# The second product for tiles 0 and 1 of the first unit: seven block products instead of eight, with the weights' block sums made earlier and in other places

## The chip, the cores and the metric

The kernel runs on one NeuronCore of one Trainium2 chip. The core has five engines with queues of their own: TensorE (PE in the profile; PEld is its weight load) multiplies matrices into PSUM, VectorE (DVE), ScalarE (ACT) and GpSimd (POOL) work elementwise, and SyncE (SP) mostly issues transfers. Each queue runs in its written order: an instruction that waits holds all behind it. The metric is the device time of one execution in microseconds (us), as the median of several runs.

## The reference

The input holds q, k and v of 8 batches, 12 heads, 448 rows and 64 columns. Attention without a softmax is followed by a feed-forward layer:

```python
scores = scale * np.matmul(q, k.transpose(0, 1, 3, 2))
attn = np.maximum(scores, 0.0) ** 2 / S
x = matmul(attn, v)              # heads side by side: B x 448 x 768
xn = (x - mu) / np.sqrt(var + 1e-06) * g_ln
out = x + np.maximum(xn @ w_ch1, 0.0) @ w_ch2     # 768 -> 3072 -> 768
```

All is given and returned in float32; the kernel multiplies in bf16.

## The kernel before, in words

**Attention.** A batch is done in three periods, n = 3 b + 0..2, of four heads each. A period has seven score steps s = 0..6 (`att_QK`, L584: four matmuls of 64x448 into one of three PSUM slots), a relu that empties the slot (L593 on ScalarE or L595 on VectorE), a square in place (L608 on VectorE, L610 on POOL), and then AV (`att_AV`, L645, 28 matmuls), whose result is copied as x transposed (L363 on ScalarE, L365 on VectorE). POOL adds x up for the mean (`sum_part`, L734 to L737), one matmul with ones makes the mean (`center`, L816), ScalarE saves it (L829), and VectorE subtracts it (L837) and applies the gain (L846; ScalarE L844).

**First product of the layer, `ffn_1`.** 24 steps for a batch, each six matmuls of 128x448 (L926) into one of two PSUM banks. A relu writes h (L942 on ScalarE, L944 on VectorE). For the second batch (b = 1) each relu is two instructions, of 64 and 384 columns, since part of h lies in a buffer called A (its first half, for tiles 4 to 6) and B (its second).

**Second product.** A unit is two batches, 896 rows in seven tiles of 128; tile 3 takes rows of both batches. For a tile `ffn_2` does two column halves of 384, each a sum of 24 matmuls of 128x384 (L1212), which VectorE drains with the row's scale and the residual x (L1230) and ScalarE's queue stores. The first unit's tiles are all done so, in the order 4, 5, 6, 3, 0, 1, 2, after `ffn_1` of the second batch, with the attention of batch 2 (periods 6 to 8; below: one to three) put in between.

In later units the pairs (0, 1), (3, 4) and (5, 6) use seven block products instead of eight (`ffn_w`, L1122): h of two tiles is a 2 x 2 block matrix a11..a22 (tile by half of the 3072), w2 one of b11..b22. Each product is 12 matmuls of 128x384, made in the order P1 = a11 b11, P2 = a12 b21, P6 = S2 T2, P5 = S1 T1, P7 = S3 T3, P3 = S4 b22, P4 = a22 T4. The S are differences of h, made for each pair by VectorE (`s_op`, L1079: S3 = a21 - a11 in place, S2 = a22 - S3 in a home of its own, S1 and S4 in place of a11 and a12), two instructions each. The T are sums of w2's blocks, made once (`make_sums`, L989: T3 = b22 + b12, T2 = T3 - b11, T4 = b21 - T2, T1 = b12 - b11), 12 blocks of 384 columns each. The order of the drains (L1130) is fixed by the sums they make: P1, P2, P6, P5, P7, P3 and P4 each have one.

Homes in the kernel before: T3 and the first two blocks of T2 in buffer A, the rest of T2 in the freed v buffer and the freed input of `ffn_1` of batch 0 (`v0`, `xc0`), T4 in `xc0`, behind the transposed x (`xT_all`) and in `x_all[:, 6]`, which is tile 2's residual; T1 in the k half of the staging buffer `stage["cols"]` and at the end of `at_all`. S2 lies in `x_all[:, 4:6]`, the residual of tiles 0 and 1.

**What sets the order.** Every operation goes to `Order`, a planner in the kernel's text. It has a modelled cost and wait for each operation; TensorE's order is set by `segment`, which interleaves steps of the layer with visits of attention, and the other engines' operations are placed in modelled time by readiness and then by `key` (lower first). An operation with two engines goes to the one that would end it first. What results is a fixed queue for each engine; on the chip nothing is reordered. `hooks` in `segment` are calls made when a given step is reached: loads of batch 3 at step 0, its transposes (`turn_qk`, SP, L414) and `make_sums` at step 24 + 32, that is after four tiles. POOL's queue also issues the loads of q, k (L401) and v (L385), SP's the transposes of x (L764). `later` and `now_known` name an operation that is added afterwards.

Of the kernel before, what the change touches and what calls it, by code (L numbers as in the profile page):

```python
# [199 lines left out]
def kernel(  # L200
# [10 lines left out]
    nc = tc.nc  # L211
    P = 128
# [5 lines left out]
    B, H, S, D = q.shape  # L218
# [15 lines left out]
    FIRST_ORDER = "qqaqaqqqqqqaaaqaqaaqaqaqqqaaaqaaqaaqqaaqqaaaaaaaa"  # L234

# [156 lines left out]
    def load_qk_cols(b):  # L392

        free = [ops["qk_free", 0]] if b == 2 else [later("turn", b - 1, x) for x in range(2)]
        for t, src in enumerate((q, k)):
# [588 lines left out]
    def make_sums():  # L984

        def run(o, i0, i1, sub, deps, key):
            def emit(eng):
                e = nc.vector if eng == "DVE" else nc.gpsimd
                (e.tensor_sub if sub else e.tensor_add)(o, i0, i1)  # L989
            n = o.shape[1] * hd  # L990
            return R.add(("DVE", "POOL"), (100.0 + 0.55 * n, 120.0 + 2.05 * n), emit, deps, key=key, port=True)

        wide = lambda t, n: t.rearrange("p (k c) -> p k c", c=hd)[:, :n]
        homes = []
        a_t = big_pool.tile([P, BIG], bf16, tag="A")
        v_t = v_pool.tile([P, H // 2, S], bf16, tag="v0")
        c_t = xc_pool.tile([P, K1, S], bf16, tag="xc0")
        homes = [(a_t[:, :14 * hd], 14, [ops["f2_end", 1]]),
                 (v_t.rearrange("p a c -> p (a c)"), 7, []), (c_t.rearrange("p a c -> p (a c)"), 7, []),
                 (xT_all[:, 4 * d_model:], 6, [ops[x, bb] for x in ("x_read", "turn_x") for bb in range(2)]),  # L1000
                 (x_all[:, 6, :], 2, [later("f2_out", 0)])]
        space = [(v.rearrange("p (k c) -> p k c", c=hd)[:, i:i + 1], d) for v, n, d in homes for i in range(n)]
        free = [(v.rearrange("p (k c) -> p k c", c=hd), n, d) for v, n, d in homes]
        made = {}

        def place(name):

            k, out = 0, []
            while k < KH:
                v, n, d = free.pop(0)  # L1010
                w = min(n, KH - k)
                out.append((k, v[:, :w], d))
                for i in range(w):
                    tw[name, k + i] = v[:, i]
                if w < n:
                    free.insert(0, (v[:, w:], n - w, d))
                k += w
            return out

        def pieces(runs):  # L1020
            for k, v, d in runs:
                n = v.shape[1]
                for i in range(0, n, 3):
                    yield k + i, v[:, i:min(i + 3, n)], d
        t3, t2, t4 = place("T3"), place("T2"), place("T4")
        w2_ld = [ops["w2", K2 - 1]]
        for k, o, d in pieces(t3):
            made["T3", k] = run(o, b22[:, k:k + o.shape[1]], b12[:, k:k + o.shape[1]], False, w2_ld + d, 5.0)
        done3 = [op for (x, _), op in made.items() if x == "T3"]
        for k, o, d in pieces(t2):  # L1030
            for i in range(o.shape[1]):
                made["T2", k + i] = run(o[:, i:i + 1], tw["T3", k + i].rearrange("p (o c) -> p o c", o=1),
                                        b11[:, k + i:k + i + 1], True, done3 + d, 5.1)
        for k, o, d in pieces(t4):
            for i in range(o.shape[1]):
                made["T4", k + i] = run(o[:, i:i + 1], b21[:, k + i:k + i + 1],
                                        tw["T2", k + i].rearrange("p (o c) -> p o c", o=1), True, [made["T2", k + i]] + d, 5.2)
        at_end = at_all[:, (N_AT - 1) * 2 * S:].rearrange("p (k c) -> p k c", c=hd)
        for a, z in ((0, 3), (3, 5), (5, J), (J, 10), (10, KH)):
            o = stage["cols"][:, 1, a:z] if a < J else at_end[:, a - J:z - J]  # L1040
            for k in range(a, z):
                tw["T1", k] = o[:, k - a]
            made["T1", a] = run(o, b12[:, a:z], b11[:, a:z], True, w2_ld + [later("turn", 3, 1), later("av_done", 1)], 5.3)
        for name in ("T1", "T2", "T3", "T4"):
            ops["sums", name] = [op for (x, _), op in made.items() if x == name]

    s2_t = x_all[:, 4:6, :].rearrange("p m (k c) -> p (m k) c", c=P)
# [21 lines left out]
    def s_op(u, m, name, part, deps):  # L1069
# [3 lines left out]
        a1, a2 = tile_cols(u, m), tile_cols(u, m + 1)  # L1073
        a11, a12, a21, a22 = h1[:, k, a1], h1[:, k_hi, a1], h1[:, k, a2], h1[:, k_hi, a2]
# [7 lines left out]
    def pair_start(u, m):  # L1082
# [5 lines left out]
        for part in range(2):  # L1088
            e["S2"].append(s_op(u, m, "S2", part, [e["S3"][part], later("h", b, KH + (part + 1) * KH // 2 - 1),
                                                   later("s2_free", u, m), later("f2_out", 0)]))  # L1090

    def ffn_w(u, m, name, part):
# [13 lines left out]
        if final and name == "P4":  # L1106
            last_product(u, m, part, e, r2, deps)
            return
# [411 lines left out]
```

## Time and profile before

| | |
|---|---|
| median of 5 runs | 525.45 us (525.43 to 525.57) |
| the profiled execution's own time | 525.45 us |
| its span, first to last instruction | 523.6 us |
| TensorE busy | 510.7 us, 98% of the span, 4104 matmuls |
| VectorE, ScalarE, POOL busy | 348.8, 220.3, 115.8 us |
| granted TensorE clock | 0.999 of full speed |

Two readings help with what follows. A matmul's duration in a row (326 ns for 128x384) is longer than its pace, because matmuls overlap; the chain's pieces give the pace. And an engine's instructions overlap a little too: two squares of 0.61 us each take 1.15.

### The profile page before, as it was taken

How to read it: one execution, taken by the hardware profiler on the slowest of the kernel's cores; microseconds unless marked ns; L12 is line 12 of the kernel's file. 1: busy time of each engine (PE TensorE's matmuls, PEld its weight loads, DVE VectorE, ACT ScalarE, POOL GpSimd, SP SyncE). 2: the span in 40 equal slices, each digit the busy share in tenths (PEclk: the TensorE clock that was granted, in tenths of full speed). 3: DMA queues.
4: the chain of work that ended last, by engine and by line, in shares of the span. 5: the costliest groups of instructions: out<-in, count | busy, mean ns of one | idle time of the engine just before them, and what ended most of it. 6: DMA issues, size and time to landing. Idle time of an engine off the chain costs nothing.

```text
span 523.6 us, 9887 instructions
## 1 busy us (share of the span) xinstructions
PE 510.7 (98%) x4104; PEld 277.1 (53%) x4104; DVE 348.8 (67%) x647; ACT 220.3 (42%) x350; POOL 115.8 (22%) x130
## 2 busy tenths in 40 slices
PE   5899999999999999999999999999999999999996
PEld 3444455555555455554555545554556545555564
DVE  5988647538996768774888667748597666634253
ACT  5977611115404663265422664346531466114300
POOL 6421600401263112321250311503221002100000
PEclk9999999999999999999999999999999999999999
DMA  9999999996299901999059960989224400242022
GB/s 188 197 188 194 199 189 165 172 126 108 61 154 146 102 2 19 165 127 106 15 103 113 125 78 15 150 111 100 41 46 88 88 1 0 54 78 22 2 60 62
DMA packets 144281, 51.83 MB, mean 99 GB/s; under 512 B 121830, under 2 KB 142188, under 8 KB 144236
## 3 DMA queue, kind: packets, MB, share of 16 engines
q0 software_dynamic: 81072, 25.50, 45.9%
q1 hardware_dynamic: 55804, 14.79, 18.6%
q10 hardware_dynamic: 7360, 10.92, 8.6%
q8 instruction: 32, 0.52, 0.4%
q14 instruction: 13, 0.11, 0.1%
HBM read 51.91 MB, written 11.01 MB: 120 GB/s over the span
## 4 chain that ended last, share of the span: by engine, by line
PE 95%; DVE 2%; ACT 1%; DMA 1%; issue 0%; ACTq 0%; DVEq 0%
PE f_ps L926 42%; PE f_ps L1122 23%; PE f_ps L1212 15%; PE sc L584 7%; PE ps L645 5%; DVE at_all L608 1%; ACT at_all L593 1%; DVE t L365 1%; DMA f<-in_q_dram 1%; PE ps L504 1%; PE f_ps L906 0%; PE f_ps L1187 0%; PE ps L707 0%; PE f_ps L504 0%; PE slot L816 0%
## 5 line engine op out<-in xcount | busy, mean ns | idle before, releaser
L926 PE MATMUL f_ps<-a,w 128*128 128x448 bf16 x1134 | 220.6, 353 | 0.0
L926 PEld LDWEIGHTS <-w 128*128 128x128 bf16 x1134 | 108.2, 98 | 107.2 <-issue 9.4
L593 ACT ACTIVATE at_all<-sc 128x896 bf16<-128x896 f32 x109 | 95.9, 924 | 78.8 <-PE sc L584 71.9
L942 ACT ACTIVATE h<-f_ps 128x448 bf16<-128x448 f32 (+1 forms) x157 | 83.6, 533 | 107.2 <-PE f_ps L926 105.7
L608 DVE TENSOR_TENSOR at_all<-at_all 128x896 bf16<-128x896 bf16 x158 | 99.5, 666 | 1.9 <-ACT at_all L593 1.8
L1122 PEld LDWEIGHTS <-h 128*128 128x128 bf16 x636 | 61.5, 98 | 42.7 <-issue 2.2
L595 DVE TENSOR_SCALAR at_all<-sc 128x896 bf16<-128x896 f32 x50 | 54.4, 1088 | 42.5 <-PE ps L645 23.2
L1212 PE MATMUL f_ps<-w,h 128*128 128x384 bf16 x336 | 56.3, 326 | 0.0
L1122 PE MATMUL f_ps<-w,h 128*128 128x384 bf16 x324 | 56.2, 326 | 0.0
L584 PE MATMUL sc<-t 64*64 64x448 bf16 x672 | 49.1, 366 | 3.0 <-DVE t L365 1.5
L1212 PEld LDWEIGHTS <-h 128*128 128x128 bf16 x336 | 32.4, 98 | 22.6 <-issue 1.5
L736 POOL TENSOR_TENSOR sum_t<-sum_t,xT_all 128x384 f32<-128x384 f32 (+2 forms) x25 | 21.5, 861 | 86.3 <-ACT xT_all L363 86.3
L584 PEld LDWEIGHTS <-t 64*64 64x64 bf16 x672 | 18.6, 107 | 27.7 <-issue 19.1
L1130 DVE SCALAR_TENSOR_TENSOR o_all<-f_ps,r_t,x_all 128x384 f32<-128x384 f32 x35 | 21.5, 614 | 16.8 <-PE f_ps L1122 16.5
L401 POOL DMA_DIRECT2D t<-in_k_dram x12 | 20.0, 1902 | 50.6 <-DMA t<-t 50.6
L645 PE MATMUL ps<-at_all,v_t 64*64 64x448 bf16 x552 | 29.8, 350 | 0.0
L734 POOL TENSOR_TENSOR sum_t<-xT_all 128x384 f32<-128x384 bf16 (+2 forms) x13 | 11.2, 906 | 84.1 <-ACT xT_all L363 83.9
L1230 DVE SCALAR_TENSOR_TENSOR o_all<-f_ps,r_t,x_all 128x384 f32<-128x384 f32 x20 | 12.3, 613 | 24.6 <-PE f_ps L1212 24.6
L363 ACT CAST xT_all<-ps 128x768 bf16<-128x768 f32 (+2 forms) x31 | 19.7, 641 | 21.2 <-PE ps L645 13.3
L645 PEld LDWEIGHTS <-v_t 64*64 64x64 bf16 x672 | 19.7, 107 | 13.4 <-issue 2.8
L401 POOL DMA_DIRECT2D t<-in_q_dram x12 | 19.3, 1772 | 31.3 <-DMA t<-t 30.0
L1130 DVE SCALAR_TENSOR_TENSOR o_all<-f_ps,r_t,o_all 128x384 f32<-128x384 f32 x27 | 16.6, 615 | 13.7 <-PE f_ps L1122 13.6
(98 smaller groups left out, 420.8 us busy)
## 6 DMA issues: line engine op xcount, KB each, us to landing
out_dram<-o_all ACTq DMA_DIRECT2D x70, 96.0 KB, 2.2
v_t<-in_v_dram POOLq DMA_DIRECT2D x16, 336.0 KB, 6.4
w<-in_moe_w_ch_dram POOLq DMA_DIRECT2D x4, 1152.0 KB, 38.5
t<-in_q_dram POOLq DMA_DIRECT2D x12, 336.0 KB, 8.3
t<-in_k_dram POOLq DMA_DIRECT2D x12, 336.0 KB, 6.8
out_dram<-o_all ACTq DMA_DIRECT2D x20, 192.0 KB, 4.6
w<-in_moe_w_ch_dram POOLq DMA_DIRECT2D x4, 768.0 KB, 19.1
w<-in_moe_w_ch_dram POOLq DMA_DIRECT2D x1, 1536.0 KB, 28.8
```

The costliest lines, as they stand in the source:

```text
L401: nc.gpsimd.dma_start(stage["cols"][half * T:(half + 1) * T, t if b < 4 else 0].rearrange("p j (h d) -> p j h d", d=D), src[b, half * 6:ha ...
L584: nc.tensor.matmul(sc[rows_of(half), r, :S], qkT[b][rows_of(r), 1, s * NPER + pn, rows_of(half)], qT[:, :, pn, rows_of(half)], start=True, ...
L593: nc.scalar.activation(attn[n, s], st[0][:, :, :S], Act.Relu, scale=rc2)
L595: nc.vector.tensor_scalar(attn[n, s], st[0][:, :, :S], rc2, 0.0, op0=Alu.mult, op1=Alu.max)
L608: nc.vector.tensor_mul(attn[n, s], attn[n, s], attn[n, s])
L645: nc.tensor.matmul(av_st[n][half][rows_of(hh)], vt[b][rows_of(half), 2 * pn + hh, s * D:(s + 1) * D], attn[n, s][rows_of(half), hh, :], st ...
L736: nc.gpsimd.tensor_add(s0, s0, x0)
L926: nc.tensor.matmul(st[0], w1[:, ki, ni * P:(ni + 1) * P], xc[b][:, ki, :], start=(i == 0), stop=(i == K1 - 1))
L942: nc.scalar.activation(o, st[0][:, c], Act.Relu)
L1122: nc.tensor.matmul(e["ps", bank], a(k), w(k), start=new and k == 0, stop=k == KH - 1, skip_group_check=True)
L1130: nc.vector.scalar_tensor_tensor(o, e["ps", bank], r, o if more else xm[u, m + tile_n][:, cols], op0=Alu.mult, op1=Alu.add)
L1212: nc.tensor.matmul(o_st["ps"], stat(u, m, ki), w2[:, ki, j * hd:(j + 1) * hd], start=(ki == 0), stop=(ki == K2 - 1))
```

## The change: what it does

1. Tiles 0 and 1 of the first unit are done as a pair with seven products, after tiles 4, 5, 6, 3 and 2. `pair_start(0, 0)` adds S3 and S2 at step 24 + 24, after tile 6.
2. The T are made in two parts. Part 0 is added at step 12 of `ffn_1` of the second batch: T3 in `v0` and `xc0`, T1's last five blocks, T2's first eight (one in each of those buffers, six behind `xT_all`). Part 1 is added after tile 6: T2's last four in buffer A, T1's other seven in the staging buffer's k half, T4's first ten in A and two in tile 2's residual. Keys are 5.0 and 1.0. A piece of T2 waits only for its own blocks of T3.
3. S2 of the first unit lies in the q half of the staging buffer, so it waits for batch 3's first transpose, and the load of q for batch 4 waits for the last reader of that S2 (`"s2 used"`).
4. Batch 3's transposes and buffer A's reuse wait for tile 6 (`f2_end`, 1) instead of tile 3.

What the built queues show of it: TensorE has 4092 matmuls. In `ffn_1` of the second batch, ScalarE does 11 of the 24 relu pairs (6 before), VectorE 13; VectorE makes T3, three blocks of T1 and one of T2 there, POOL two of T1 and seven of T2. In the stretch after it VectorE has two pieces of T2, ten of T4 and three instructions of T1, POOL two of T2 and two of T4; one copy of x transposed (768 columns) is on VectorE instead of ScalarE, three relus of scores are on ScalarE instead of VectorE. POOL has one square (L613 in the new numbering) between batch 4's loads of q and k. SP's order is the same.

The diff, with part of the old `make_sums` left out:

```diff
--- before.py
+++ after.py
@@ -232,6 +232,7 @@
     N_FILL = 8
 
     FIRST_ORDER = "qqaqaqqqqqqaaaqaqaaqaqaqqqaaaqaaqaaqqaaqqaaaaaaaa"
+    SUM_KEY = (5.0, 1.0)
 
     HELD = {(13, 0): -2, (15, 0): -1, (16, 0): 3, (19, 0): 4, (21, 0): -1, (22, 0): 3}
     SUMMED = [0] + [2] + [NPER] * (B - 2)
@@ -392,6 +393,8 @@
     def load_qk_cols(b):
 
         free = [ops["qk_free", 0]] if b == 2 else [later("turn", b - 1, x) for x in range(2)]
+        if b == 4:
+            free.append(later("s2 used", 0))
         for t, src in enumerate((q, k)):
             ld = []
             for half in range(2):
@@ -981,70 +984,73 @@
     b11, b12 = w2[:, :KH, :hd], w2[:, :KH, hd:]
     b21, b22 = w2[:, KH:, :hd], w2[:, KH:, hd:]
 
-    def make_sums():
...
-        a_t = big_pool.tile([P, BIG], bf16, tag="A")
-        v_t = v_pool.tile([P, H // 2, S], bf16, tag="v0")
-        c_t = xc_pool.tile([P, K1, S], bf16, tag="xc0")
-        homes = [(a_t[:, :14 * hd], 14, [ops["f2_end", 1]]),
-                 (v_t.rearrange("p a c -> p (a c)"), 7, []), (c_t.rearrange("p a c -> p (a c)"), 7, []),
-                 (xT_all[:, 4 * d_model:], 6, [ops[x, bb] for x in ("x_read", "turn_x") for bb in range(2)]),
-                 (x_all[:, 6, :], 2, [later("f2_out", 0)])]
...
-        t3, t2, t4 = place("T3"), place("T2"), place("T4")
-        w2_ld = [ops["w2", K2 - 1]]
...
-        at_end = at_all[:, (N_AT - 1) * 2 * S:].rearrange("p (k c) -> p k c", c=hd)
-        for a, z in ((0, 3), (3, 5), (5, J), (J, 10), (10, KH)):
-            o = stage["cols"][:, 1, a:z] if a < J else at_end[:, a - J:z - J]
-            for k in range(a, z):
-                tw["T1", k] = o[:, k - a]
-            made["T1", a] = run(o, b12[:, a:z], b11[:, a:z], True, w2_ld + [later("turn", 3, 1), later("av_done", 1)], 5.3)
...
-    s2_t = x_all[:, 4:6, :].rearrange("p m (k c) -> p (m k) c", c=P)
+    sums = {x: {} for x in ("T1", "T2", "T3", "T4")}
+
+    def blocks(t, n):
+        return t.rearrange("p (k c) -> p k c", c=hd)[:, :n]
+
+    def make_sum(name, k, o, deps, key):
+
+        n = o.shape[1]
+        for i in range(n):
+            tw[name, k + i] = o[:, i]
+        w = slice(k, k + n)
+        prev = {"T1": [], "T3": [], "T2": "T3", "T4": "T2"}[name]
+
+        def emit(eng):
+            e = nc.vector if eng == "DVE" else nc.gpsimd
+            if name == "T3":
+                e.tensor_add(o, b22[:, w], b12[:, w])
+            elif name == "T1":
+                e.tensor_sub(o, b12[:, w], b11[:, w])
+            else:
+                for i in range(n):
+                    x = tw[prev, k + i].rearrange("p (o c) -> p o c", o=1)
+                    y = slice(k + i, k + i + 1)
+                    if name == "T2":
+                        e.tensor_sub(o[:, i:i + 1], x, b11[:, y])
+                    else:
+                        e.tensor_sub(o[:, i:i + 1], b21[:, y], x)
+        if prev:
+            deps = deps + [sums[prev][k + i] for i in range(n)]
+        m = n if prev else 1
+        op = R.add(("DVE", "POOL"), (100.0 * m + 0.55 * n * hd, 120.0 * m + 2.05 * n * hd), emit,
+                   [ops["w2", K2 - 1]] + deps, key=key, port=True)
+        for i in range(n):
+            sums[name][k + i] = op
+        ops["sums", name] = list(sums[name].values())
+
+    def make_sums(part):
+
+        if part == 0:
+            v_t = v_pool.tile([P, H // 2, S], bf16, tag="v0")
+            c_t = xc_pool.tile([P, K1, S], bf16, tag="xc0")
+            v_b, c_b = (blocks(t.rearrange("p a c -> p (a c)"), J) for t in (v_t, c_t))
+            x_b = blocks(xT_all[:, 4 * d_model:], 6)
+            x_free = [ops[x, bb] for x in ("x_read", "turn_x") for bb in range(2)]
+            at_end = blocks(at_all[:, (N_AT - 1) * 2 * S:], 5)
+            todo = [("T3", 0, v_b[:, 0:3], []), ("T3", 3, v_b[:, 3:6], []), ("T3", 6, c_b[:, 0:3], []), ("T3", 9, c_b[:, 3:6], []),
+                    ("T1", 7, at_end[:, 0:3], [later("av_done", 1)]), ("T1", 10, at_end[:, 3:5], [later("av_done", 1)]),
+                    ("T2", 0, v_b[:, 6:7], []), ("T2", 1, c_b[:, 6:7], []),
+                    ("T2", 2, x_b[:, 0:2], x_free), ("T2", 4, x_b[:, 2:4], x_free), ("T2", 6, x_b[:, 4:6], x_free)]
+        else:
+            a_t = big_pool.tile([P, BIG], bf16, tag="A")
+            a_b = blocks(a_t, 14)
+            cols = stage["cols"][:, 1]
+            gone, turned = [ops["f2_end", 1]], [later("turn", 3, 1)]
+            todo = ([("T2", k, a_b[:, k - 8:k - 6], gone) for k in (8, 10)]
+                    + [("T1", a, cols[:, a:z], turned) for a, z in ((0, 3), (3, 5), (5, 7))]
+                    + [("T4", k, a_b[:, k + 4:k + 6], gone) for k in (0, 2, 4, 6, 8)]
+                    + [("T4", 10, blocks(x_all[:, 6, :], 2), [later("m2_out")])])
+        for i, (name, k, o, deps) in enumerate(todo):
+            make_sum(name, k, o, deps, SUM_KEY[part] + 0.01 * i)
+
+    s2_home = x_all[:, 4:6, :].rearrange("p m (k c) -> p (m k) c", c=P)
+
+    def s2_of(u):
+
+        return stage["cols"][:, 0].rearrange("p j c -> p (j c)")[:, :KH * P].rearrange("p (k c) -> p k c", c=P) if u == 0 else s2_home
+
     PRODUCTS = ("P1", "P2", "P6", "P5", "P7", "P3", "P4")
     ws = {}
 
@@ -1071,6 +1077,7 @@
         k = slice(part * KH // 2, (part + 1) * KH // 2)
         k_hi = slice(KH + k.start, KH + k.stop)
         a1, a2 = tile_cols(u, m), tile_cols(u, m + 1)
+        s2_t = s2_of(u)
         a11, a12, a21, a22 = h1[:, k, a1], h1[:, k_hi, a1], h1[:, k, a2], h1[:, k_hi, a2]
         o, i0, i1 = {"S3": (a21, a21, a11), "S2": (s2_t[:, k], a22, a21), "S1": (a11, a11, s2_t[:, k]),
                      "S4": (a12, a12, s2_t[:, k])}[name]
@@ -1087,7 +1094,7 @@
             e["S3"].append(s_op(u, m, "S3", part, [later("h", b, (part + 1) * KH // 2 - 1)] ))
         for part in range(2):
             e["S2"].append(s_op(u, m, "S2", part, [e["S3"][part], later("h", b, KH + (part + 1) * KH // 2 - 1),
-                                                   later("s2_free", u, m), later("f2_out", 0)]))
+                                                   later("s2_free", u, m)]))
 
     def ffn_w(u, m, name, part):
 
@@ -1106,6 +1113,7 @@
         if final and name == "P4":
             last_product(u, m, part, e, r2, deps)
             return
+        s2_t = s2_of(u)
         bank = "x" if name in ("P1", "P6", "P7", "P4") else "y"
         w = {"P1": lambda k: b11[:, k], "P2": lambda k: b21[:, k], "P6": lambda k: tw["T2", k], "P5": lambda k: tw["T1", k],
              "P7": lambda k: tw["T3", k], "P3": lambda k: b22[:, k], "P4": lambda k: tw["T4", k]}[name]
@@ -1148,6 +1156,8 @@
                 now_known(s2_last, "s2_free", u, 5)
             elif m == 5 and u < B // 2 - 1:
                 now_known(s2_last, "s2_free", u + 1, 0)
+            elif u == 0:
+                now_known(s2_last, "s2 used", 0)
             elif m == 0:
                 now_known(s2_last, "s2_free", u, 3)
         elif name == "P5":
@@ -1166,9 +1176,8 @@
             o_done[e["turn"]][0] = store_tile(u, m + 1, lo, ev, False, e["o", 0])
             if m == 3:
                 ops["m3_out", u] = e["C12"]
-            elif m == 5:
+            elif m == 5 or u == 0:
                 now_known(ev, "f2_out", b)
-                now_known(op, "f2_end", b)
 
     def last_product(u, m, part, e, r2, deps):
 
@@ -1212,9 +1221,7 @@
                 nc.tensor.matmul(o_st["ps"], stat(u, m, ki), w2[:, ki, j * hd:(j + 1) * hd],
                                  start=(ki == 0), stop=(ki == K2 - 1))
         op = R.pe(975.0 * 4 / parts, emit, f2_deps(u, m, j, part, parts))
-        if m in (2, 6) and j == 1 and part == parts - 1:
-            now_known(op, "f2_end", b)
-        if (u, m) == (0, 3) and j == 1 and part == parts - 1:
+        if (u, m) == (0, 6) and j == 1 and part == parts - 1:
             ops["f2_end", 1] = op
         if part < parts - 1:
             return
@@ -1232,7 +1239,9 @@
         ev = R.add("DVE", 620.0, evac, [op, ops["rstd", b], o_done[turn][j]], key=-3.0)
         f_use(ev)
         if j == 1:
-            if m in (2, 6):
+            if (u, m) == (0, 2):
+                now_known(ev, "m2_out")
+            elif m in (2, 6):
                 now_known(ev, "f2_out", b)
             if m == 3:
                 ops["m3_out", u] = ev
@@ -1468,8 +1477,10 @@
         for n in range(2 * NPER, 3 * NPER):
             vis += period(n, n > 2 * NPER, False)
         vis.append(av_of(3 * NPER - 1))
-        segment(f1_steps(1) + f2_steps(0, (4, 5, 6, 3, 0, 1, 2)), vis, 2, 9000.0,
-                hooks=[(0, lambda: load_batch(3, False)), (K2 + 8 * PARTS, lambda: turn_qk(3)), (K2 + 8 * PARTS, make_sums)])
+        now_known(later("turn", 3, 0), "s2_free", 0, 0)
+        segment(f1_steps(1) + f2_steps(0, (4, 5, 6, 3, 2)) + fw_steps(0, [0]), vis, 2, 9000.0,
+                hooks=[(0, lambda: load_batch(3, False)), (K2 // 2, lambda: make_sums(0)), (K2 + 6 * PARTS, lambda: turn_qk(3)), (K2 + 6 * PARTS, lambda: make_sums(1)),
+                       (K2 + 6 * PARTS, lambda: pair_start(0, 0))])
         for b in range(2, B):
             u = b // 2
             vis = []
@@ -1481,7 +1492,7 @@
                 vis += [period(n0 + NPER, True, False)[0]] if b + 2 < B else [av_of(n0 + NPER - 1)]
             hooks = [(0, lambda b=b: load_batch(b + 2))] if b + 2 < B else []
             if b == 2:
-                now_known([], "s2_free", 1, 0)
+                now_known(later("f2_out", 0), "s2_free", 1, 0)
             f2 = fw_steps(u, [0]) + f2_steps(u, [2]) if b % 2 == 0 else fw_steps(u, [3, 5])
             for m in [0] if b % 2 == 0 else [3, 5]:
                 pair_start(u, m)
```

## The prediction

> **What bounds the kernel now.** I read the page's shares first, then the chain that ended last, then the stretch that the change rewrites (113 to 162 us) engine by engine.
>
> ```profile
> span 523.6 us, 9887 instructions
> PE 510.7 (98%) x4104; PEld 277.1 (53%) x4104; DVE 348.8 (67%) x647; ACT 220.3 (42%) x350; POOL 115.8 (22%) x130
> PE 95%; DVE 2%; ACT 1%; DMA 1%; issue 0%; ACTq 0%; DVEq 0%
> ...
> 96.28 17.55 PE f_ps L1212 x108
> ...
> 120.32 0.62 DVE L608 TENSOR_TENSOR at_all<-at_all 128x896 bf16<-128x896 bf16 x1 [0.18 <-ACT at_all L593]
> 131.09 0.92 ACT L593 ACTIVATE at_all<-sc 128x896 bf16<-128x896 f32 x1 [2.97 <-PE sc L584]
> 131.47 1.09 DVE L595 TENSOR_SCALAR at_all<-sc 128x896 bf16<-128x896 f32 x1 [1.36 <-PE ps L645]
> 134.53 1.40 POOL L737 TENSOR_TENSOR sum_t<-sum_t,xT_all 128x384 f32<-128x384 f32 x1
> 134.54 1.87 DVE L608 TENSOR_TENSOR at_all<-at_all 128x896 bf16<-128x896 bf16 x2
> 144.81 2.47 POOL L736 TENSOR_TENSOR sum_t<-sum_t,xT_all 128x384 f32<-128x384 f32 x1
> ...
> 143.15 7.91 PE f_ps L1212 x48
> 151.06 0.19 PE slot L816
> 151.25 9.75 PE f_ps L1212 x60
> 161.00 0.69 PE sc L584 x12
> ...
> 121.60:131.00 9.40, 9.40 (x101) 5.18 (x104) 8.28 (x13) 4.26 (x5) 1.52 (x2) 1.00 0.97 153
> 131.00:141.60 10.60, 10.60 (x104) 5.82 (x92) 10.13 (x15) 4.53 (x6) 3.26 (x4) 1.00 0.29 71
> 141.60:151.00 9.40, 9.40 (x78) 5.54 (x78) 9.40 (x27) 0.97 (x2) 7.04 (x8) 1.00 0.76 100
> ...
> w<-in_moe_w_ch_dram POOLq DMA_DIRECT2D x1, 1152.0 KB, 46.2
> ```
>
> TensorE is on 95% of the chain and, in the stretch that matters, on all of it: its pieces follow each other without a hole. So a matmul less is worth its pace, and a stall costs its whole length. The pace is not the 326 ns of a row (matmuls overlap) but 17.55 us / 108 = 162.5 ns; each return from attention to block products adds 0.11 (12 matmuls take 2.06 instead of 1.95). The three window rows (columns: PE, PEld, DVE, ACT, POOL) show what can turn against the change: VectorE is busy 27.8 of 29.4 us there, while ScalarE has 20 us free.
>
> **Products.** Tiles 0 and 1 took 2 tiles x 2 halves x 24 = 96 matmuls; seven products of 12 are 84. Twelve fewer at 162.5 ns: **-1.95 us**, all on the path. The built order has 4092 matmuls instead of 4104. Attention visits are the same in number (two of them come 6 or 12 matmuls later), so no 0.11 is added. Without a stall, TensorE in after reaches (from the pieces above): the fourth score of the third period at 133.75, the mean at 149.12, P6 149.31, P5 151.26, P7 153.21, P3 155.16, P4 157.11, the next scores at 159.05 (161.00 before). From there its sequence is the old one but for the names of the homes.
>
> **Sums begun in ffn_1 of the second batch.** VectorE gives five of its 18 relu pairs there to ScalarE, which then does 11 of 24 (0.22 + 0.49 us each, a step takes 6 x 0.19 = 1.14). In their place stand four T3 (0.744 each), a T1 (0.747) and a T2 (0.34). T3 needs w2: its last load was issued at 35.10 and landed 46.2 later, at 81.3; the T3 that reads it stands where about 87.4 comes out (first statistics end 83.43, T3 to 84.2, two more statistics of 1.25, T3 to 87.35). VectorE must be back for its next relu pair at 90.65: 87.4 + 2 x 0.70 + 0.70 + 0.34 = 89.8. Two PSUM banks give 0.4 more. POOL makes a T1 (768 wide: no row; between 0.91 for 384 and twice that) and seven T2 of 0.912, and its next load, for batch 3, waited until 97.93 before; T2 starts at 84.3 and ends near 94. Cost 0; bounds 0 to 0.5 (one POOL sum of 0.91 ahead of a T3, less the 0.4).
>
> **VectorE from 113 to 162.** Added: eight differences S1 to S4 (0.55, 4.4 us), three more drains (0.614, 1.8), one x^T copy of 768 that ScalarE did (no row; between 0.618 for 448 and 1.09 for 896 I take 0.95). Gone: sums, 31 instructions of 13.3 us, of which ten T4 and two T2 (0.34) and three T1 (0.75 + 2 x 0.55) remain, 5.9; three score relus of 1.09 go to ScalarE. Net 4.4 + 1.8 + 0.95 - 7.4 - 3.3 = -3.6 us. So the load falls, but sums that filled holes late now stand ahead of work that TensorE waits for. The queue, by the paces of the rows (square 0.535, sum 0.28, drain 0.54):
> - To the third period's second score relu on VectorE's queue. AV of period one ends as before, so the copy starts at 123.98 (ScalarE's copy did); + 0.87 + 7 squares 3.75 + 12 sums 3.36 + drain 0.54 = 132.50, relu to 133.6. It stood at 131.47 before. That relu frees the slot for the fourth score, due at 133.75: margin 0.1, which one delayed square eats. Cost **0.2**; bounds 0 and 0.75, the pair beside POOL (1.87 instead of 1.15) having lost 0.72.
> - After it the queue waits for TensorE again (last drain of tile 2 at 145.25), so a lag does not pile up. The squares for AV of period three end at 141.05, needed from 141.7.
> - P1 ends 147.1: drain 147.8, S1 148.75, T1 149.25, P2's drain 149.8, S4 150.7, one xc difference 151.6, P6's drain 152.2. P5 (151.26) needs S1, T1 and P2's drain; P7 (153.21) needs P6's drain: margin 1.0. POOL's two T4 (0.91 each) fall on S1 and S4. Cost 0; bounds 0 and 0.4 (two losses of 0.72 less 1.0).
> - P3 needs P5's drain (153.9) and S4; P4 P7's (155.9); ffn_1 of batch 2 at 159.7 needs the gains, done by 157.3.
>
> **Waits and queues.** The mean needs POOL's last x sums: AV ends 143.16, two v loads 1.34, then 0.91 + 0.91 + 0.42 + 0.30 = 147.2 to 148.7 (2.47 instead of 0.91, the row at 144.81), due 149.12: cost 0, bound 0.3. T4's last two wait behind these sums, 149.5 to 150.9, due 157.1. The load of q for batch 4 now waits for S2's reader, P6 (151.3; 149.35 before); queued behind it are a square of batch 3 (ScalarE's relu after 165.9; AV from about 178.5), k's load (167.1 before, about 169 after) and later x sums and v. Batch 4's k transpose (in SP's row of 18.5 us from 160.16, so started near 175 before) then starts near 178 and lands near 184; batch 4's first scores come at 203.4 (with AV at 205.4 before). Transposes of batch 3 start at tile 6's end (121.7) instead of tile 3's (125.80 in SP's rows), nothing behind them is late, and S2's home, the q columns, is free by 131, needed at 141. Eight stores of 96 KB for four of 192: four more issues on ScalarE, 0.56 each by pairs of 1.12, in a stretch where it worked 2.0 of 10.6 us. Cost 0.
>
> **A rule against the row.** Row: two squares took 1.87 instead of 1.15 beside a POOL sum, but the two at 125.72 took 1.26 beside another, and it was POOL that took 2.47 for 0.91 while VectorE ran without a gap. The Trainium skill, SBUF — State Buffer, section "SBUF: two separate sides", calls the shared port pair an exclusive lock, kept for a whole instruction, the loser blocked; it speaks against sums on POOL. By the rule alone, with VectorE always the loser, the result would be that of the second rival below, 527.6; the trace shows both losing, so I keep the rows.
>
> **Sum.** 525.45 (the profiled execution's own time: 523.6 span and 1.85 around it; equal to the median of the five runs) - 1.95 + 0.2 = **523.7**.
>
> **Rivals.**
> - Half or more of the gain is stalled away (a gain under 1.05). All upper bounds together, 0.75 + 0.5 + 0.4 + 0.3 = 1.95, return everything: 525.45; two thirds of them give 524.8. For it: margins of 0.1 and 1.0 on a queue 94% busy. Against: the bounds need a POOL collision at every place. Chance 0.18.
> - Slower, by the port pair: from 121.7 to 132.5 POOL runs two T2 (0.91 each) and two x sums (0.91 + 0.67), and later two T4. If every one holds VectorE for its length, the relu comes 3.4 late (less 0.1: 3.3) and P7 0.8: 525.45 - 1.95 + 4.1 = 527.6. It decides from 3.0 of stall (over 0.2% slower). For it: the row at 134.54. Against: drains, relus and copies from PSUM ran beside POOL at 1.09 and 0.61, and the pair at 125.72 lost 0.1. Chance 0.06.
> - w2's last load as the limit: landed 91 or later instead of 81.3 it would hold T3, VectorE's relu pairs and so TensorE past the whole gain. Nothing before it is changed; counted in the two above. That the change removes nothing is excluded by the built order.
>
> **How the numbers follow.** A change of 0.2% (1.05 us) is about what a measurement of this kernel can tell from none: 524.4 and 526.5 are the borders. Forecast 0.76, all of it faster; first rival 0.18, same; second 0.06, slower. Lower end: no stall and 0.3 less in switches and waits now there (three of 0.11), 523.2. Upper: into the first rival, 525.0, leaving out about 0.1 above.
>
> **What would show it.** Right: 4092 matmuls; the next scores at 159 to 159.4; chain without VectorE in the stretch; the rest shifted by the same 1.8. Wrong: a wait of TensorE on L595's relu before the third period's fourth score, on P6's drain before P7, or on relu pairs near 91 us.

## The result and the profile after

The changed kernel takes **526.33 us** (median of 23 runs, 526.01 to 528.37) where the kernel before took 525.55 (43 runs, 525.39 to 527.76): a ratio of **1.0016, 95% interval 1.0009 to 1.0022**. So it is slower by 0.8 us, within the 0.2% called no change, and 1.3 us above the range that was given. Its profiled execution took 526.22 us.

First the page's lines on span, busy time and the chain's shares, and one row of windows, 121.60 to 131.00 us (columns: length, then PE, PEld, DVE, ACT, POOL, each with its number of instructions). Lines of the kernel are shifted: L1221 is the half products (1212 before), L1130 the block products (1122), L929 `ffn_1` (926), L587 the scores, L598 their relu on VectorE, L1003 T3, L1005 T1, L1011 T2, L1013 T4, L1086 the differences S, L1138 the pair's drains.

```profile
span 524.4 us, 9897 instructions
PE 509.5 (97%) x4092; PEld 275.7 (53%) x4092; DVE 349.3 (67%) x635; ACT 224.3 (43%) x361; POOL 128.6 (25%) x142
PE 90%; DVE 6%; ACT 1%; issue 1%; DMA 1%; ACTq 0%; DVEq 0%
121.60:131.00 9.40, 8.49 (x90) 4.57 (x88) 9.40 (x17) 5.35 (x7) 3.02 (x3) 1.00 0.89 162
```

The twelve matmuls are gone and TensorE is 1.2 us less busy, but VectorE, 2% of the chain before, now holds 6% of it, and TensorE stands idle 0.9 us in this window. The chain (start, length, what) names the places:

```profile
92.16 4.71 PE f_ps L929 x24
96.87 17.55 PE f_ps L1221 x108
...
124.16 1.01 DVE at_all L598
125.17 0.04 issue
125.21 0.38 PE sc L587 x4
...
147.02 1.96 PE f_ps L1130 x12
...
154.81 0.54 DVE o_all L1138
...
155.40 2.11 PE f_ps L1130 x12
...
157.54 4.06 PE f_ps L1130 x24
161.60 0.69 PE sc L587 x12
```

Batch 3's first scores come at 161.60 (161.00 before, 159.05 forecast): the twelve matmuls gave their 1.95 and 2.55 were lost. From there on everything is 0.60 later than before; the other 0.2 of the span (524.4 against 523.6) lies behind the last drain, which ends at 520.70 (520.10 before). The 2.55 by place:

| place | lost, us | read from |
|---|---|---|
| `ffn_1` of the second batch, near 92 | 0.59 | tile products at 96.87, before 96.28 |
| period two's second score relu, near 125 | 1.03 | the scores at 125.21 |
| two small waits, near 127.6 and 135.2 | 0.19 | 0.07 and 0.12: twelve score matmuls take 0.76 instead of 0.69, eight 0.57 instead of 0.45 |
| the pair's end, 147 to 161.6 | 0.74 | 14.58 from P1 to the scores; 84 products of 0.1625 and the mean's 0.19 make 13.84 |

The timeline of VectorE and POOL at the three large places shows what they share: in each, both engines run two-input instructions with all sides in SBUF.

```profile
87.00 2.13 DVE L1003 TENSOR_TENSOR c_t<-w 128x1152 bf16<-128x1152 bf16 x2
89.06 1.46 DVE L1005 TENSOR_TENSOR at_all<-w 128x1152 bf16<-128x1152 bf16 x1
90.44 1.06 DVE L1011 TENSOR_TENSOR c_t<-v_t,w 128x384 bf16<-128x384 bf16 x1
91.42 0.21 DVE L947 TENSOR_SCALAR h<-f_ps 128x64 bf16<-128x64 f32 x1
87.12 4.17 POOL L1011 TENSOR_TENSOR xT_all<-v_t,w 128x384 bf16<-128x384 bf16 x3 [1.20 <-issue]
91.25 1.89 POOL L1011 TENSOR_TENSOR xT_all<-c_t,w 128x384 bf16<-128x384 bf16 x2
...
120.48 2.26 POOL L1011 TENSOR_TENSOR a_t<-c_t,w 128x384 bf16<-128x384 bf16 x2 [15.41 <-PE f_ps L1221]
120.91 1.07 DVE L611 TENSOR_TENSOR at_all<-at_all 128x896 bf16<-128x896 bf16 x1 [0.18 <-ACT at_all L596]
121.90 1.73 DVE L1086 TENSOR_TENSOR h<-h 128x768 bf16<-128x768 bf16 x2
124.08 1.07 DVE L598 TENSOR_SCALAR at_all<-sc 128x896 bf16<-128x896 f32 x1
...
149.51 2.09 POOL L1013 TENSOR_TENSOR x_all<-w,a_t 128x384 bf16<-128x384 bf16 x2
149.54 2.48 DVE L1086 TENSOR_TENSOR h<-h,t 128x768 bf16<-128x768 bf16 x2
152.41 0.61 DVE L1138 SCALAR_TENSOR_TENSOR o_all<-f_ps,r_t,o_all 128x384 f32<-128x384 f32 x1
156.87 0.62 DVE L1138 SCALAR_TENSOR_TENSOR o_all<-f_ps,r_t,x_all 128x384 f32<-128x384 f32 x1 [0.66 <-DMA out_dram<-o_all]
```

A T2 of 384 columns takes VectorE 0.34 alone and took 1.06; S1's pair takes 1.01 and took 2.48. TensorE's rows for the pair show two waits behind it:

```profile
150.94 0.33 PE L1130 MATMUL f_ps<-v_t,t 128*128 128x384 bf16 x1
...
153.07 1.30 PE L1130 MATMUL f_ps<-t,h 128*128 128x384 bf16 x7
...
155.40 1.14 PE L1130 MATMUL f_ps<-v_t,h 128*128 128x384 bf16 x6 [0.22 <-DVE o_all L1138]
```

P6 starts at 150.94 and P5 2.13 later instead of 1.95, just as P2's drain ends (152.41 + 0.61): 0.17 lost. P7 follows 2.33 behind P5, when P6's drain ends: 0.38 lost. The last VectorE row above is something else: P5's drain waited 0.66 for the store of tile 2, whose buffer it overwrites, and P3 starts 0.19 late by it. These three are the 0.74.

### The profile page after: what moved, and what is told of

The parts are those of the page before. It is cut to its first block, busy times and chain, and to the rows that moved or that the text cites. A ratio compares the mean times of both kernels' runs of the same rounds, so it can differ in the third digit from the quotient of the medians.

```text
span 524.4 us, 9897 instructions
## 1 busy us (share of the span) xinstructions
PE 509.5 (97%) x4092; PEld 275.7 (53%) x4092; DVE 349.3 (67%) x635; ACT 224.3 (43%) x361; POOL 128.6 (25%) x142
## 4 chain that ended last, share of the span: by engine, by line
PE 90%; DVE 6%; ACT 1%; issue 1%; DMA 1%; ACTq 0%; DVEq 0%
PE f_ps L929 40%; PE f_ps L1130 25%; PE f_ps L1221 11%; PE sc L587 7%; PE ps L648 5%; DVE at_all L611 1%; ACT at_all L596 1%; DVE t L366 1%; DMA f<-in_q_dram 1%; DVE h L1086 1%; PE ps L507 1%; PE f_ps L909 0%; DVE c_t L1003 0%; DVE at_all L598 0%; PE f_ps L1196 0%
## 5 line engine op out<-in xcount | busy, mean ns | idle before, releaser
L929 PE MATMUL f_ps<-a,w 128*128 128x448 bf16 x1134 | 220.7, 353 | 0.4 <-DVE t L947 0.4
L929 PEld LDWEIGHTS <-w 128*128 128x128 bf16 x1134 | 108.2, 98 | 107.8 <-issue 9.4
L596 ACT ACTIVATE at_all<-sc 128x896 bf16<-128x896 f32 x112 | 98.4, 924 | 79.2 <-PE sc L587 72.2
L945 ACT ACTIVATE h<-f_ps 128x448 bf16<-128x448 f32 (+1 forms) x162 | 84.7, 523 | 106.0 <-PE f_ps L929 104.6
L1130 PEld LDWEIGHTS <-h 128*128 128x128 bf16 x708 | 68.5, 98 | 48.1 <-issue 3.2
L598 DVE TENSOR_SCALAR at_all<-sc 128x896 bf16<-128x896 f32 x47 | 51.1, 1087 | 41.2 <-PE ps L648 21.5
L1130 PE MATMUL f_ps<-w,h 128*128 128x384 bf16 x360 | 62.3, 326 | 0.0
L587 PE MATMUL sc<-t 64*64 64x448 bf16 x672 | 49.3, 365 | 4.0 <-DVE t L366 1.5
L739 POOL TENSOR_TENSOR sum_t<-sum_t,xT_all 128x384 f32<-128x384 f32 (+2 forms) x25 | 19.9, 796 | 88.8 <-ACT xT_all L364 88.8
L1221 PE MATMUL f_ps<-w,h 128*128 128x384 bf16 x240 | 40.5, 326 | 0.0
L1138 DVE SCALAR_TENSOR_TENSOR o_all<-f_ps,r_t,x_all 128x384 f32<-128x384 f32 x39 | 24.0, 615 | 18.9 <-PE f_ps L1130 17.9
L587 PEld LDWEIGHTS <-t 64*64 64x64 bf16 x672 | 18.7, 106 | 29.1 <-issue 20.9
L1221 PEld LDWEIGHTS <-h 128*128 128x128 bf16 x240 | 23.0, 98 | 16.2 <-issue 1.3
L1138 DVE SCALAR_TENSOR_TENSOR o_all<-f_ps,r_t,o_all 128x384 f32<-128x384 f32 x30 | 18.4, 614 | 13.7 <-PE f_ps L1130 13.6
L386 POOL DMA_DIRECT2D v_t<-in_v_dram x16 | 10.7, 673 | 59.5 <-PE sc L587 46.0
```

The costliest lines, as they stand in the source:

```text
L587: nc.tensor.matmul(sc[rows_of(half), r, :S], qkT[b][rows_of(r), 1, s * NPER + pn, rows_of(half)], qT[:, :, pn, rows_of(half)], start=True, ...
L596: nc.scalar.activation(attn[n, s], st[0][:, :, :S], Act.Relu, scale=rc2)
L598: nc.vector.tensor_scalar(attn[n, s], st[0][:, :, :S], rc2, 0.0, op0=Alu.mult, op1=Alu.max)
L739: nc.gpsimd.tensor_add(s0, s0, x0)
L929: nc.tensor.matmul(st[0], w1[:, ki, ni * P:(ni + 1) * P], xc[b][:, ki, :], start=(i == 0), stop=(i == K1 - 1))
L945: nc.scalar.activation(o, st[0][:, c], Act.Relu)
```

## The experiments

Theory 1: POOL's sums block VectorE's operations on SBUF, and at three places what is blocked stands ahead of something TensorE waits for. Theory 2: VectorE's queue is simply too full there, whatever POOL does. Theory 3: the store is the loss behind the pair. Every ratio is against runs of the kernel before on the same chip; it is taken from all runs and can differ a little from the quotient of two medians.

### POOL's sums as memsets

In `emit` of `make_sum`:

```diff
-            if name == "T3":
+            if eng == "POOL":
+                for i in range(n):
+                    nc.gpsimd.memset(o[:, i:i + 1], 0.0)
+            elif name == "T3":
```

> The changed kernel with every sum that POOL makes (two pieces of T1, nine of T2, two of T4) replaced by a POOL memset of the same block, so that POOL reads nothing there; the sums of these pieces, and so part of the output, are left out. The queues of TensorE, VectorE and ScalarE are those of the changed kernel, instruction by instruction. Theory of the shared port (POOL's sums and VectorE's two-input sums and squares take turns, each turn costs VectorE about 0.72): T3, S3 and S1 go back to their own durations (0.74, 0.55, 0.55), the three stalls of 0.59, 1.03 and about 0.4 go, the scores after the pair start at 159.1 to 159.6 and the time is 523.5 to 524.2. Rival, a VectorE queue that is too full with so much put ahead of it: the durations do not matter, the scores stay at 161.6 and the time at 526.0 to 526.4.

POOL's sums are left out here, so the output is not the layer's. Measured: **523.86 us** (10 runs), ratio 0.9967, interval 0.9958 to 0.9977. The rows of the same three places in this kernel's timeline:

```profile
89.02 0.35 DVE L1014 TENSOR_TENSOR c_t<-v_t,w 128x384 bf16<-128x384 bf16 x1
90.64 0.23 DVE L947 TENSOR_SCALAR h<-f_ps 128x64 bf16<-128x64 f32 x1 [1.27 <-PE f_ps L929]
...
119.86 0.77 POOL L1004 MEMSET a_t<- 128x384 bf16 x2 [14.64 <-ACT at_all L596]
120.86 1.02 DVE L1089 TENSOR_TENSOR h<-h 128x768 bf16<-128x768 bf16 x2
122.44 1.09 DVE L598 TENSOR_SCALAR at_all<-sc 128x896 bf16<-128x896 f32 x1
...
148.07 0.77 POOL L1004 MEMSET x_all<- 128x384 bf16 x2
148.11 1.02 DVE L1089 TENSOR_TENSOR h<-h,t 128x768 bf16<-128x768 bf16 x2
154.92 0.62 DVE L1141 SCALAR_TENSOR_TENSOR o_all<-f_ps,r_t,x_all 128x384 f32<-128x384 f32 x1 [1.58 <-DMA out_dram<-o_all]
```

VectorE's instructions and their order are those of the changed kernel, and all three stalls are gone: its relu pair at 90.64 now waits for TensorE, tile products start at 96.28 and the scores come at 159.65. What is left against 159.05 is 0.4 ahead of the pair (P1 at 145.60 instead of 145.22), all of it at period three's second score relu, and 0.2 in the pair, behind the store. That relu stands behind four squares that took 3.04 beside POOL's sums of x (124.68 to 126.54), which no memset replaces; at the 0.535 of a square they would take 2.2. Theory 2 falls for the three places. The forecast of 523.7 was, nearly, the time of this kernel.

### One pair at a time

The same edit for T2's last pair alone (`key < SUM_KEY[0] and name == "T2"`):

> Only the two pieces of T2 that POOL makes after tile 6 (into buffer A, 120.5 to 122.7 in the changed kernel) become memsets; their sums are left out. Port theory: the square and the two S3 beside them take 0.6 and 1.0 instead of 1.07 and 1.73, the relu that the fourth score of that period waits for ends 1.0 to 1.2 earlier, TensorE's stall of 1.03 there goes, all later pieces start 1.0 earlier: 525.0 to 525.2. Full-queue rival: no difference.

525.63 in one run: the stall near 125 is gone, the other two are there (scores at 160.98, in an execution that was already 0.4 late at 62 us). The same edit for the last two T4 (`name == "T4"`):

> Only the last two pieces of T4 (POOL, beside S1 and P1's drain, 149.5 to 151.6) become memsets; their sums are left out. Port theory: the two S1 take 1.0 instead of 2.48, P6's drain comes 1.0 to 1.4 earlier and P7 starts 0.3 to 0.4 earlier: 525.6 to 525.9. If instead P5's drain, which waited 0.66 for a store of its buffer, sets the pair's end, the scores after it gain only 0.2 and the time is 525.9 to 526.1. Full-queue rival: no difference.

**527.61** in one run: a miss. S1's pair took its 1.01 and P6's drain came early, but P5's drain then waited for the store:

```profile
148.33 9.79 DMA out_dram<-o_all
...
158.25 0.62 DVE L1141 SCALAR_TENSOR_TENSOR o_all<-f_ps,r_t,x_all 128x384 f32<-128x384 f32 x1 [3.37 <-DMA out_dram<-o_all]
```

P3 starts 2.0 late by it. So the store's landing (9.8 us here, 8.0 in the chain of the kernel with all memsets) is a wait of its own, mostly hidden behind P6's drain in the changed kernel's profile (0.19 came through).

### Part 0 on one engine

The engines of a sum are pinned by its key. On POOL:

```diff
-        op = R.add(("DVE", "POOL"), (100.0 * m + 0.55 * n * hd, 120.0 * m + 2.05 * n * hd), emit,
+        engs, costs = ("DVE", "POOL"), (100.0 * m + 0.55 * n * hd, 120.0 * m + 2.05 * n * hd)
+        only = "POOL" if key >= SUM_KEY[0] else None
+        if only:
+            costs = costs[engs.index(only)]
+            engs = only
+        op = R.add(engs, costs, emit,
```

> All eleven pieces of part 0 (T3, T1's last five, T2's first eight) on POOL alone, in ffn_1 of the second batch, where VectorE keeps only relus from PSUM and statistics; the rest is the changed kernel with the same order of TensorE. Output whole. Port theory: nothing on VectorE contends there, the stall of 0.59 goes and the later ones of 1.03 and 0.4 stay: 525.4 to 525.6. Full-queue rival: VectorE has 4.1 us less in that stretch, so the 0.59 goes as well; this run tells only that the place is worth 0.59. If POOL's 21 us of sums end after its load of q for batch 3 was due (97.3), that load comes late by up to 3 us, with 10 to spare.

**527.59** (5 runs), ratio 1.0036, 1.0023 to 1.0050: a miss, though the stall near 92 is gone. The planner, given other costs, wrote other queues further on: POOL also got a T1 of 768 columns at the pair, S1's pair took 2.87 beside it, and P5's drain was placed behind three xc differences and two gains. On VectorE (`"DVE" if key >= SUM_KEY[0] else None`), which leaves TensorE's and ScalarE's queues as they are:

> Part 0 of the sums all on VectorE (it adds a T1 of 768 columns, 0.55, and seven T2, 0.28 to 0.34 each: some 2.7 us between its relu pairs); the queues of TensorE and ScalarE are those of the changed kernel. Port theory: the stall near 92 us is gone, the tile products start at 96.3 instead of 96.87, the rest unchanged: 525.7. Rival that VectorE is simply full in ffn_1 of the second batch: a relu pair comes late again, products at 96.9 or later, 526.3 or more.

**525.36** (10 runs), ratio 0.9998, 0.9987 to 1.0010, that is 0.97 below the changed kernel. From the start of `ffn_1`'s long stretch to the tile products it is 34.19 us (62.46 to 96.65), as before (62.09 to 96.28), against 34.79. VectorE does all of part 0 and is in time. The other 0.4 isn't seen: from there to P1 the stretch is the changed kernel's 50.15 to the hundredth, and the profiled execution was a long one, with a store of 9.46 us on the chain (P3 1.1 late).

### Eight products with the early sums

Tiles 0 and 1 are done with `ffn_2`, in the order 4, 5, 6, 3, 2, 0, 1; no `pair_start(0, 0)`, all sums as in the changed kernel.

> The sums made early and in the new homes, as in the changed kernel, but tiles 0 and 1 with eight block products: what the sums cost without the seven products' gain. Port theory: before plus the stalls near 92 (0.6) and near 125 (about 1.0), 526.7 to 527.3. Rival that the stalls belong to the pair (its differences and drains on VectorE): 525.4 to 525.8.

**526.54** (10 runs), ratio 1.0023, 1.0013 to 1.0033. The stall near 92 is there (0.61, and the scores come at 161.67), the one near 125 is not: a miss by half. POOL's T2 pair runs at 120.57 as before and stretches a square to 1.07, yet the relu is in time, since S3's pair isn't ahead of it. It needs both.

### S3 behind the relu

```diff
-            e["S3"].append(s_op(u, m, "S3", part, [later("h", b, (part + 1) * KH // 2 - 1)] ))
+            e["S3"].append(s_op(u, m, "S3", part, [later("h", b, (part + 1) * KH // 2 - 1)] + ([later("S3 late")] if u == 0 else [])))
...
         slot_use(ev)
+        if (n, s) == (7, 1):
+            now_known(ev, "S3 late")
```

> The changed kernel with S3's pair held behind the score relu that it stood ahead of near 122 us (period two's second); all sums where they were, T2's pair on POOL too (some squares change places behind it, and one copy of x transposed goes back to ScalarE). Theory that the stall near 125 is S3's pair on VectorE, stretched by POOL's two T2 from 1.0 to 1.7: it falls to 0 to 0.3, the stall near 92 stays, 525.3 to 525.7. Rival that POOL's T2 alone make it (the square is stretched too): the stall stays over 0.6, 526.0 or more.

**525.37** (10 runs), ratio 0.9991, 0.9982 to 1.0001: 0.96 below the changed kernel, about as much as that stall was long (1.03). With this the second place is settled from four sides: with S3 ahead and T2 on POOL 1.03; with either of them away (memsets, eight products, S3 behind) nothing. And with part 0 on VectorE as well:

> The same and part 0 of the sums on VectorE alone: both places are cleared, only the pair's end is left as it was. Theory, by the stalls as measured one by one: 526.3 - 0.6 - 0.7 to 1.0 = 524.7 to 525.0, faster than before. Rival that one stall hid another (a queue that is full further on): 525.3 or more.

**525.03** (10 runs), ratio **0.9983, 0.9974 to 0.9993**; profiled execution 524.20. By the medians this is 1.3 us below the changed kernel, and the interval lies below the kernel before as well. Its chain has no VectorE ahead of the tile products and a full run of eight scores at 121.7. Two stalls are left: 0.3 at period three's second score relu (P1 at 145.51 instead of 145.22) and 0.56 at the pair:

```profile
96.28 17.55 PE f_ps L1228 x108
...
121.70 0.50 PE sc L587 x8
...
132.84 1.01 DVE at_all L598
...
133.89 0.38 PE sc L587 x4
...
145.51 1.96 PE f_ps L1137 x12
...
153.89 6.01 PE f_ps L1137 x36
159.90 0.69 PE sc L587 x12
```

### The store, and the pair's end

Tile 2's column halves in the other order, each stored by itself; no other queue changes. The diff in part:

```diff
...
+        if (u, m) == (0, 2):
+            o_done[turn][j] = store_tile(u, m, slice(j * hd, (j + 1) * hd), ev, False, o_all[:, turn])
...
```

> Tile 2's two column halves in the other order, each stored by itself (96 KB stores, the second half's issued before the first half's work); the queues of TensorE, VectorE, POOL and SyncE are those of the changed kernel. P5's drain writes over the half whose store now leaves some 4 us earlier. Theory that the store wait is a small part of the loss (0.2 to 0.5 us, now and then 1 to 3): 525.8 to 526.2 and less spread, no VectorE piece with a DMA as releaser after the pair's P6. Rival that the store wait is most of the loss behind the pair: 525.4 or less.

**526.42** (10 runs), ratio 1.0008, 0.9996 to 1.0020: the wait has left the chain (scores at 161.45, 0.15 earlier), and P5 and P7 are as late as before (0.56 together). The median has not moved, and the two ratios' intervals overlap. Theory 3 falls: the store is the small part of the loss at the pair. With the two edits before:

> S3's pair late, part 0 on VectorE, and tile 2 in two stored halves; the other queues as in the run with the late S3 and part 0 on VectorE. If the store's landing makes the spread of that run (524.2 to 526.1, median 525.0): 524.2 to 524.4 and no piece of the chain that is a store. If it does not: the same spread.

**524.91** (10 runs, 524.29 to 526.84), ratio 0.9989, 0.9976 to 1.0002. The spread is as wide as without the halves, so the store doesn't make it alone. For one pair of executions the profiles show what does: this kernel was profiled twice (again in the repeat that gave 525.27, below), at 524.47 and 525.62, and the second is 1.16 behind already where `ffn_1`'s long stretch starts (63.39 against 62.23), before anything that the change touches. Its chain begins with a load of k for the first batch that landed 6.7 us after its issue, against 4.0 in the other. For the other executions it stays open.

> S3's pair late, part 0 on VectorE, and POOL's last two T4 wait for S4 (one wait more, all queues the same): they fall beside the differences of xc instead of S1. Port theory: S1's pair takes 1.0 instead of 2.5, P6's drain comes 1.4 earlier and does not hold P7; 0.2 to 0.4 less than without the wait, unless the store holds P5's drain. Rival that VectorE's own queue makes P6's drain late: no gain.

> Both together: all three places cleared and the store wait gone. Next scores at 159.6 to 159.8, 523.7 to 524.1; the best of all if the stalls add up as measured.

These two told something else than they were meant to. The wait stood in the planner's list alone; it changed no queue and no semaphore, so they are the two kernels above once more: **524.54** (10 runs), ratio 0.9982, 0.9972 to 0.9992, without the halves, and **525.27** (11 runs), 0.9984, 0.9976 to 0.9993, with them. The better version stands twice, at 0.17% and 0.18% below the kernel before. One and the same kernel has medians of 525.03 and 524.54 here, and the one with halves 524.91 and 525.27, so a difference of half a microsecond between medians of ten runs tells nothing by itself. T4 behind S4 was not tried.

Two ways of moving T4 to VectorE, too, with part 0 there and the halves stored apart, the second with S3 and S2 added twelve steps later:

> Part 0 and the last two T4 on VectorE, and tile 2 in two stored halves; S3 as in the changed kernel (TensorE's queue is that of the changed kernel, POOL makes T2's last pair and two pieces of T1). The stall near 92 and that of P6's drain go, the stall near 125 stays: 524.9 to 525.4 and P5's drain without a DMA as releaser. Rival that VectorE or the moved T1 pieces make P5 or P6's drain late again: 525.5 or more.

> Part 0 and the last two T4 on VectorE, tile 2 in two stored halves, and the pair's S3 and S2 added 12 half-product steps later, shortly before the pair. All three places cleared: 523.7 to 524.5 if VectorE has room. If its queue is what limits once the port is free, a score relu in period three or the mean comes late by 0.5 to 1.5: 524.8 to 526.

**527.87** (5 runs), ratio 1.0037, 1.0024 to 1.0050, and **525.64** (10 runs), 0.9997, 0.9988 to 1.0006. Both miss. In the first the planner gave POOL two T1 in T4's place, and S1's pair paid for them, the longest case seen:

```profile
148.82 3.55 POOL L1005 TENSOR_TENSOR t<-w 128x768 bf16<-128x768 bf16 x2
149.15 3.64 DVE L1091 TENSOR_TENSOR h<-h,t 128x768 bf16<-128x768 bf16 x2
```

In the second, a T1 of 1152 columns took 2.19 beside POOL's T1 (0.75 alone), and P5 and P4 wait 0.69 and 0.84 for drains that stand behind sums and gains. Last, all sums on VectorE, T2's last four held until period two's last square:

> All sums on VectorE, T2's last four held until the last square of period two, and tile 2 in two stored halves. POOL then touches the shared port only for the sums of x. Port theory with room on VectorE: next scores at 159.3 to 160, 523.8 to 524.6, better than before and after. If VectorE's queue is full without POOL's help (six more sums between 121 and 158, some 1.8 us): a score relu or a drain comes late by 0.5 to 1.5 and it ends at 524.8 to 526.

**525.38** (10 runs), ratio 1.0001, 0.9989 to 1.0014. The pair's end has no stall at all (13.84 from P1 to the scores, S1's pair 1.01), and with the halves alone P5 and P7 were still late, so S1's stretch is confirmed as the cause there in a kernel that leaves nothing out; but eight T4 stand ahead of a copy that frees a PSUM slot, and period three starts late:

```profile
122.97 2.14 DVE a_t L1015 x8
125.11 0.54 DVE at_all L611
125.65 0.21 DVE xT_all L366
125.86 0.04 issue
125.90 0.38 PE sc L587 x4
```

So all sums don't fit on VectorE either, where the planner puts them: theory 2 has a part in what can be reached, though it was not seen at the three places where the change lost.

## Why the prediction was wrong

**Right.** The products: 12 x 162.5 ns = 1.95. The mean, the loads, SP's queue and w2's landing cost nothing. The step that was watched most, period three's second score relu, forecast at 0.2 (0 to 0.75), cost 0.12. That was partly luck: TensorE came to it 1.7 us late by the stalls before, and with these gone (memsets) it cost 0.4, since the count of VectorE's queue took nothing for the four squares that lost 0.8 beside POOL's sums of x.

**The step that failed** is the rule against the row: "the trace shows both losing, so I keep the rows". From a row in which POOL was the loser I took it that a loss beside POOL would be small and shared, and added it up only as bounds. The rows right behind that one, in the same trace of the kernel before, show the other side losing and were not read:

```profile
146.96 1.53 DVE L989 TENSOR_TENSOR c_t<-w,v_t 128x384 bf16<-128x384 bf16 x2
147.36 0.91 POOL L737 TENSOR_TENSOR rsum_t<-sum_t,xT_all 128x384 bf16<-128x384 f32 x1
```

Two VectorE sums took 1.53 there instead of 0.61. The runs show that in the places that count VectorE lost: some 0.7 for most of its two-input instructions that met a POOL sum of 0.91. The Trainium skill, SBUF — State Buffer, section "SBUF: two separate sides", had said that the port pair is held for a whole instruction and the loser blocked. The rows agree (S1's first half starts at 149.54 and lasts 1.29 instead of 0.55, beside a POOL sum from 149.51 to 150.41), and without POOL's sums nothing is lost (S1's pair 1.02). What was not held back stands below. By term:

- **Sums in `ffn_1`**, cost 0 (0 to 0.5): 0.59. The bound took one POOL sum ahead of a T3. In fact POOL's T2 start as soon as the first T3 is there and alternate one for one with T3, T1 and T2 on VectorE: three losses of 0.7, against the 1.27 us that VectorE is idle there with memsets on POOL, and the second PSUM bank.
- **A step left out**: the count of VectorE's queue began with "AV of period one ends as before, so the copy starts at 123.98". Ahead of that copy stands period two's second score relu, and ahead of the relu, new, S3's pair; the sum had no term for it. The rival had POOL begin T2 at tile 6's end, 121.7; it began at 120.48, released by a matmul of tile 6 before its last (the last twelve of a sum of 24 read h from buffer B). A square and S3's pair lost 0.45 and 0.71, and 1.03 of it came through.
- **P6's drain**, cost 0 (0 to 0.4): 0.55, by the mechanism that the bound described, though both T4 fell on S1 and none on S4 (1.47 lost; the bound took 1.44). With memsets P2's drain ends 1.31 before P5 is due and P6's 0.93 before P7. So 0.17 came through at P5, which had no price, and 0.38 more at P7.
- **Stores**, cost 0: counted as issues on ScalarE only. That P5's drain writes over tile 2's buffer was in `ffn_w`'s list of waits and not followed: P3 was 0.19 late in this profile, 0.3 with the late S3, 1.1 with part 0 on VectorE, 2.0 with T4 as memsets. Together with P6's drain this is the pair's 0.74.

Of the three signs of being wrong that the prediction names, two were seen (relu pairs near 91, P6's drain before P7); the largest stall was at a place that it doesn't name.

Against the rivals: the second had the mechanism, chance 0.06, and put its price in the wrong places, 3.3 at period three's relu and 0.8 at the pair, 4.1 in all where 2.55 came. The outcome is the first rival's class (same) with the second's cause; its upper bounds, 1.95 together, assumed that the losses were bounded by what the trace before showed at places where POOL had little to do. The margins were the warning: with 0.1 and 1.0 us of slack and 0.72 per collision in the rows at hand, every new POOL sum had to be laid beside VectorE's queue, one by one.

## What to carry to other kernels

Sums moved to POOL "beside" VectorE are not beside it when both read and write SBUF: price each at what VectorE loses, about 0.7 us for a POOL instruction of 0.9, and look only at what stands on VectorE's queue in that very stretch ahead of something TensorE waits for. Holding back the work that isn't due (here S3, first read 20 us later, by S2 at 142.69) cleared its place as well as taking POOL's work away did. And a wait in a planner's list is no wait on the chip: read the built queues and the data each instruction touches, buffers being stored from included.

## What the runs showed of the hardware

- VectorE's bf16 operations with two SBUF inputs and POOL's take turns, instruction by instruction: S1's pair took 1.01 alone, 2.48 beside two POOL sums of 384 (2.09), 3.64 beside two of 768 (3.55).
- Not held back, while POOL made its T2 pair from 91.25 to 93.14: VectorE's relus out of PSUM (0.21 and 0.54) and the statistics (0.54). POOL's memsets (0.77 for two) hold nothing: S1's pair beside them took 1.02.
- Who loses varies: before the change POOL took 2.47 for 0.91 beside a run of twelve VectorE sums, and next to its following sum (0.91) two VectorE sums took 1.53 instead of 0.61. No run was made to tell what decides it.
- In the kernel with S3 and S2 twelve steps later, two gains of VectorE took 2.11 (0.58 alone) and ended when POOL had issued q's loads (155.12, 3.22 long); a difference of xc (128x384) beside the same issue kept its 0.54. In another kernel four gains that began at 157.88, with such an issue lasting to 158.16, took 1.10, hardly more than elsewhere (1.07). It was seen once and not followed.
- The same store of tile 2 landed in 8.0, 8.6, 9.5 and 9.8 us in executions of four of these kernels.
